# Top-32 attention and an expert layer: row scores as float32 products of two row halves, candidates in blocks, a new list

## The chip, the cores and the metric

The kernel runs on one core of a Trainium2 chip. The metric is the device time of one execution in microseconds, the median of several. TensorE (PE in the profile) multiplies, VectorE (DVE) finds the top 32, ScalarE (ACT) copies out of PSUM and computes exponentials, GpSimd (POOL) does the small and slow elementwise work, SyncE (SP) issues the transfers.

## What is computed

Two stages. The first is attention for 8 batches of 8 heads, 576 rows of 64 elements, in which each row keeps only its 32 largest scores; the second is a layer of four attention experts over the result, of which each row takes two.

```
scores = q @ k.T / 8;  kth = 32nd largest of each row
scores = where(scores >= kth, scores, -1e9);  x = softmax(scores) @ v      # per batch and head
logits = x @ w_gate;  sel = the two largest of 4;  w = softmax(sel)
out += [e in sel] * w * (causal_softmax(x wq_e (x wk_e).T / 8) (x wv_e)) wo_e   # per expert e
```

Which 32 scores a row keeps depends on their order, so the row scores are computed to nearly float32 precision.

## The kernel before

Two heads make a pair, and 32 pairs are worked off, four to a batch. The two heads of a pair have x = 0 and 1. Their 1152 rows are nine tiles of 128: tiles 0 to 3 are rows of head 0, 5 to 8 of head 1, and tile 4 holds the last 64 rows of head 0 and the first 64 of head 1.

**Preparation** (`prep`, from L684). One transfer brings q (partitions 0 to 63) and k (64 to 127) of both heads into `raw`. Each half is rounded to float32r (`cast`, ScalarE), the remainder is formed in place (`sub`, GpSimd), and copies on SP's queue (`dup1`, `dup2`, `again`) lay three operands of 128 partitions: q1 = [q low; q high], k1 = [k high; k low], q2 = [q high; q low], and k2 with k high again. In the first pair head 0 is loaded once more with q and k exchanged (`load_swap`), and ScalarE and VectorE make the operands. 16 products of zeros come first on TensorE (`warm`).

**Row scores** (`scores`, L805). For a tile q1' k1 + q2' k1, each in two PSUM banks: four float32r products of 128 partitions, 576 columns twice over; tile 4 needs eight, as gaps of zeros keep the heads apart. ScalarE copies the tile out (`copy`, L809).

**Top 32** (`topk`, L790). For three tiles at once VectorE takes the maximum and minimum of the two halves of a row (`f1`, `f3`), folds the maxima twice more (`f2`, `f4`), and so makes candidates: 72 maxima, 72 minima, and three times the eight largest of what else is left (`f5`, `f6`), 168 in all. Four rounds take the eight largest (`win`) and strike them out (`rep`), two over the 72, two over the 168. GpSimd computes the smaller ones of one fold (`lesser`, L839 and L840), copies the eighth of each of the three eights to a place behind (`tails`, L852), and prepares a test whether the candidates sufficed (`compare`, L898). ScalarE makes a mask from the 32nd value (L917).

**Statistics and tail** (`stats`, `tail`). Row maximum and logarithm of the sum are split in two, transposed (`s8`, L998), and sent by SP as two more rows into q2 (`s10`, L1003). Then the scores are computed again, transposed and masked (`st`), ScalarE's exponential follows (L1105), and `av` multiplies with V in plain float32, two column halves of 64 side by side. float32 products show as two records each in the trace, the other types as one.

**Expert layer** (`moe`, L1135), once for each batch. Its stages are spread among the pairs that follow; in the score stage (`s_stage`) the two experts of a group lie in partitions 0 to 63 and 64 to 127, and their products of 64 partitions are issued in turn.

**Order.** `add` (L138) enters each step with its engine, its guessed duration in ns, what it waits for and the buffers it takes. For the main part the steps are issued in the order of `ORDER` (L287), a list of step numbers written out; so each engine works in a fixed order, and what is not ready holds up all behind it on its engine. `TURNS` (L106) is the planner's table of what it costs TensorE, in ns, to go from one shape of product to another: L is 128 by 128, C two column halves, R two partition halves, M the masks, T transpositions, F and X other cases. Buffers are rings of fixed size (`Ring`): `raw` 1, operands 3 and 2, PSUM slots 3.

## Time and profile before

| what | value |
|---|---|
| median of 3 runs | 1146.33 us (1146.16 to 1147.42) |
| the profiled execution | 1148.72 us |
| its span in the profile | 1146.9 us |
| mean granted TensorE clock | 0.976 of full speed |
| DMA | 103.49 MB, of it 35.89 MB read from HBM |

The profile comes from one execution. Its span runs from the first instruction to the last; a little lies around it. Busy times of an engine are shares of that span; a busy TensorE is not TensorE at its peak, because products are pipelined and their ends are modelled. Starts are measured, so the distance from one start to the next says what a group of products takes. A product's own duration is longer than that distance.

### The profile page before, as it was taken

To read this page: it belongs to the slowest core of one execution; us is meant where nothing else is said; L and a number is where in the kernel's file an instruction comes from. 1 tells how busy PE (TensorE), PEld (TensorE's weight loads), DVE (VectorE), ACT (ScalarE), POOL (GpSimd) and SP (SyncE) were. 2 spreads that over 40 slices of the span, in tenths; PEclk is the share of its full clock that TensorE was granted. 3 is DMA by queue.
4 is the path that set the end of the run, shared out by engine and by line. 5 is a ranking of instruction groups with operands and counts; after the bars stand their busy time and mean duration, and the time that the engine had idled before them with its cause. 6 is when DMAs were issued, how large, how long until landed. Compare 5 with 4: busy or idle time off the path is not lost.

```text
span 1146.9 us, 27854 instructions
## 1 busy us (share of the span) xinstructions
PE 1063.6 (93%) x9046; PEld 904.6 (79%) x9046; DVE 1031.7 (90%) x4518; ACT 928.5 (81%) x1900; POOL 584.1 (51%) x967
## 2 busy tenths in 40 slices
PE   4488889998999999999999999999999989999997
PEld 3366678877889788887888878897888878887885
DVE  6999999998999999999999999999999999998022
ACT  4788868897888988889789888889888888888554
POOL 3765564544655556445554555554554545653211
PEclk7698999999999999999999999999999999999999
DMA  4334333334343334333433233333532433321101
GB/s 132 105 101 109 85 84 86 79 83 104 97 115 85 84 106 114 79 101 99 106 85 103 65 106 113 97 86 93 134 90 61 111 96 98 103 68 29 37 33 46
DMA packets 57654, 103.49 MB, mean 90 GB/s; under 512 B 11870, under 2 KB 19676, under 8 KB 57500
## 3 DMA queue, kind: packets, MB, share of 16 engines
q1 hardware_dynamic: 57340, 101.32, 33.7%
q8 instruction: 74, 1.21, 0.4%
q14 instruction: 80, 0.66, 0.2%
q10 hardware_dynamic: 160, 0.30, 0.1%
HBM read 35.89 MB, written 9.50 MB: 40 GB/s over the span
## 4 chain that ended last, share of the span: by engine, by line
PE 42%; DVE 33%; ACT 10%; DMA 6%; issue 4%; POOL 2%; SPq 2%; DVEq 0%; ACTq 0%; POOLq 0%
PE slot L531 33%; PE acc L531 7%; DVE top L857 7%; DVE cand L862 7%; DVE fa L822 4%; DVE cand L844 3%; DVE fb L825 2%; DVE fc L828 2%; ACT s L809 2%; ACT mask L917 2%; DVE cand L848 1%; PE slot L1378 1%; DVE cand L849 1%; DMA raw<-in_qk_dram 1%; DVE sm L1358 1%
## 5 line engine op out<-in xcount | busy, mean ns | idle before, releaser
L839 POOL TENSOR_TENSOR fc<-fa,fc 128x432 int32<-128x432 int32 x96 | 115.6, 1204 | 307.7 <-DVE cand L834 298.5
L857 DVE MAX8 top<-cand 128x8 f32<-128x72 f32 (+1 forms) x1152 | 247.0, 270 | 0.0
L917 ACT ACTIVATE mask<-s,top 128x576 bf16<-128x576 f32 x288 | 213.2, 769 | 31.5 <-DVE top L857 31.4
L531 PE MATMUL slot<-opa,opa 128*128 128x256 f32 (+3 forms) x984 | 198.4, 322 | 26.9 <-DMA opa<-raw 12.9
L862 DVE MATCH_REPLACE8 cand<-top,cand 128x72 f32<-128x72 f32 (+1 forms) x864 | 208.5, 251 | 0.0
L809 ACT ACTIVATE s<-slot 128x576 f32<-128x576 f32 x288 | 178.6, 649 | 32.0 <-PE slot L531 31.0
L1105 ACT ACTIVATE pt<-slot 128x576 f32<-128x576 f32 x288 | 183.4, 649 | 24.7 <-PE slot L531 18.9
L531 PE MATMUL slot<-opb,opb 128*128 128x320 f32 (+1 forms) x960 | 188.1, 312 | 6.7 <-ACT pt L1105 2.2
L531 PEld LDWEIGHTS slot<-opa,opa 128*128 128x128 f32 (+1 forms) x984 | 148.1, 196 | 44.1 <-issue 21.6
L531 PE MATMUL acc<-pt,vt 128*64 128x256 f32 (+3 forms) x1152 | 177.7, 413 | 5.3 <-DMA vt<-in_vL_dram 2.8
L531 PEld LDWEIGHTS slot<-opb,opb 128*128 128x128 f32 x960 | 143.8, 193 | 20.6 <-ACT pt L1105 5.0
L531 PEld LDWEIGHTS acc<-pt,vt 128*64 128x64 f32 (+1 forms) x1152 | 104.2, 143 | 44.1 <-issue 6.7
L531 PE MATMUL slot<-negi,mask 128*128 128x128 bf16 (+3 forms) x1632 | 119.5, 216 | 1.6 <-ACT pt L1105 0.8
L840 POOL TENSOR_TENSOR fa<-fa,fc 128x432 int32<-128x432 int32 x96 | 110.1, 1147 | 7.5
L822 DVE TENSOR_TENSOR fa<-s 128x864 f32<-128x864 f32 x95 | 105.1, 1106 | 9.4 <-ACT s L809 9.2
L844 DVE MAX8 cand<-fb 128x8 f32<-128x288 f32 x288 | 112.1, 445 | 0.4
L898 POOL TENSOR_TENSOR ind<-cand,top 128x513 bf16<-128x513 f32 x96 | 101.4, 1056 | 12.9 <-ACT ind L904 10.2
L825 DVE TENSOR_TENSOR fb<-s 128x864 f32<-128x864 f32 x95 | 106.4, 1120 | 0.5 <-ACT s L809 0.5
L531 PEld LDWEIGHTS <-mask 128*128 128x128 bf16 (+1 forms) x1632 | 80.3, 101 | 28.1 <-issue 14.1
L531 PE MATMUL slot<-opa,k2a 128*128 128x256 f32 (+1 forms) x320 | 69.7, 299 | 2.9 <-DMA opa<-stat 1.9
L862 DVE MATCH_VALUE_LOAD cand<-top,cand 128x8 f32 x864 | 67.6, 78 | 4.0 <-POOL cand L852 4.0
L531 PE MATMUL slot<-opb,k2b 128*128 128x320 f32 x320 | 68.8, 296 | 1.8 <-DMA opb<-stat 1.8
(189 smaller groups left out, 2132.0 us busy)
## 6 DMA issues: line engine op xcount, KB each, us to landing
raw<-in_qk_dram SPq DMA_DIRECT2D x31, 576.0 KB
opb<-raw SPq DMA_DIRECT2D x96, 144.0 KB
opa<-raw SPq DMA_DIRECT2D x93, 144.0 KB
vt<-in_vL_dram SPq DMA_DIRECT2D x32, 320.0 KB
opb<-opb SPq DMA_DIRECT2D x64, 144.0 KB
opa<-opa SPq DMA_DIRECT2D x62, 144.0 KB
k2a<-opa SPq DMA_DIRECT2D x32, 144.0 KB
k2b<-opb SPq DMA_DIRECT2D x32, 144.0 KB
```

Source lines behind the costliest of these rows:

```text
L531: nc.tensor.matmul(o, l, r, start=start, stop=stop, skip_group_check=True)
L809: nc.scalar.activation(s3.t[:, n], sl.t[:, o0:o0 + S], AF.Copy)
L822: v.tensor_tensor(out=fa.t, in0=s3.t[:, :, 0:288], in1=s3.t[:, :, 288:576], op=OP.max)
L825: v.tensor_tensor(out=fb.t, in0=s3.t[:, :, 0:288], in1=s3.t[:, :, 288:576], op=OP.min)
L839: nc.gpsimd.tensor_tensor(out=m, in0=r, in1=m, op=OP.subtract)
L840: nc.gpsimd.tensor_tensor(out=l, in0=l, in1=m, op=OP.add)
L844: v.max(out=c.t[:, n, 160:168], in_=fb.t[:, n])
L857: v.max(out=w.top.t[0][:, j, 8 * r:8 * r + 8], in_=c.t[:, n, 0:72 if r < 2 else 168])
L862: v.match_replace(out=src, in_values=src, imm_value=LOW, in_to_replace=w.top.t[0][:, j, 8 * r:8 * r + 8])
L898: nc.gpsimd.tensor_tensor(out=ind.t[:, 513 * g:513 * g + 513].rearrange("p (a n) -> p a n", a=3), in0=c.t, in1=m32[:, js[0]:js[0] + 3, 31: ...
L917: nc.scalar.activation(w.mask[j].t, s3.t[:, n], AF.Relu, bias=w.top.t[0][:, j, 31:32], scale=-1.0)
L1105: es[j] = add("ACT", act(S), lambda sl=sl, pt=pt, o0=o0: nc.scalar.activation(pt.t, sl.t[:, o0:o0 + S], AF.Exp, scale=0.125), [a], bufs=[s ...
```

## The change

The row scores no longer use the float32r operands. q and k are loaded twice: `raw`, now one buffer for each half and three of them, holds [q; k] and, by two more transfers, [k; q]. A tile's scores are two float32 products of 64 partitions: columns 0 to 287 in partitions 0 to 63 and columns 288 to 575 in partitions 64 to 127, each into a bank of its own; tile 4 has four, for two output halves as well. They wait for the loads alone. Casts, remainders and copies are still made, for `st` alone, with fewer copies, and the two other operands lose their gaps. The first pair goes the same way as the others, with 8 products of zeros in place of 16; the load of its head 1 and of the value weights wait for steps of the first head.

The candidates lie in three blocks of 56: 24 maxima, 24 minima, an eight. The last two rounds read 55 of each block, so the eighths stay where they are, and `tails` goes. `f4` and `lesser` become two steps each, and the small GpSimd steps of the statistics (`s7`) and of the expert layer (`g7`, `diag`, `c6`) two to four, with dependences of their own; their instructions stay. `TURNS` gets a shape Z for the new products, and `ORDER` is another list. The parts of the diff that count here:

```diff
@@ -103 +103 @@ TURNS, in ns, gets these entries
+ "LZ": 92.0, "MZ": 60.0, "CZ": 60.0, "TZ": 40.0, "FZ": 90.0, "RZ": 0.0, "ZL": 42.0,
+         "ZC": 49.0, "ZT": 48.0, "ZM": 20.0, "ZR": -50.0, "ZX": 42.0, "ZF": 40.0}
@@ -285,227 +286,244 @@ ORDER: 5308 numbers become 5710, all in a new order
...
-    RAW = ring("raw", [P, 2, S], FT, int(1))
-    OPS = [sets("opa", int(3), *[([P, 640], FR)] * 3),
-           sets("opb", int(2), *[([P, 640], FR)] * 3)]
+    RAW = ring("raw", [P, 2, S], FT, 3)
+    OPS = [sets(f"op{n}", 2, ([P, S], FR), ([P, 640], FR), ([P, S], FR)) for n in "ab"]
...
-    CAND = ring("cand", [P, 3, 171], FT, 2)
-    IND = ring("ind", [P, 1548], BF, 1)
+    CAND = ring("cand", [P, 3, 3, 56], FT, 2)
+    IND = ring("ind", [P, 1521], BF, 1)
@@ -687,82 +703,66 @@
         pl.due = p - D_PREP
         w.ops, w.k2 = [Buf(r) for r in OPS], [Buf(r) for r in K2]
         w.vt = Buf(VT)
-        raw = Buf(RAW)
+        w.raw = [Buf(RAW) for _ in range(2)]
         src = qk[b, i]
-        w.scores, w.k2d = {}, []
-        load = None
+        w.loads, w.k2d = [], []
+        a = None
         for x in range(2):
-            ops, k2 = w.ops[x], w.k2[x]
+            ops, k2, raw = w.ops[x], w.k2[x], w.raw[x]
             c = slice(OFF[x], OFF[x] + S)
-            first = start and x == 0
-            if load is None or start:
-                ls = slice(x, x + 1) if start else slice(0, 2)
-                def load_(ls=ls):
-                    nc.sync.dma_start(raw.t[:, ls], src[:, ls])
-                load = add("SP", 820 if start else 1640, load_, bufs=[raw], lat=500 if start else 0, prio=1)
-            def cast(x=x, c=c):
-                nc.scalar.activation(w.ops[x].t[2][:, c], raw.t[:, x], AF.Copy)
-            def sub(x=x, c=c, first=first):
+            def load_(x=x, raw=raw):
+                nc.sync.dma_start(raw.t[:, 0], src[:, x])
+            def swap_(x=x, raw=raw):
+                eng = nc.scalar if start and x == 0 else nc.sync
+                for r, z in ((hi, lo), (lo, hi)):
+                    eng.dma_start(raw.t[r, 1], src[z, x])
+            def cast(x=x, raw=raw):
+                nc.scalar.activation(w.ops[x].t[2], raw.t[:, 0], AF.Copy)
+            def sub(x=x, raw=raw):
                 q1, k1, q2 = w.ops[x].t
-                if first:
-                    for t, r in ((q1, lo), (k1, hi)):
-                        nc.vector.tensor_tensor(out=t[r, c], in0=raw.t[r, x], in1=ft(q2[r, c]), op=OP.subtract)
-                else:
-                    nc.gpsimd.tensor_tensor(out=raw.t[:, x], in0=raw.t[:, x], in1=ft(q2[:, c]), op=OP.subtract)
+                nc.gpsimd.tensor_tensor(out=q1, in0=raw.t[:, 0], in1=ft(q2), op=OP.subtract)
             def dup1(x=x, c=c):
                 q1, k1, q2 = w.ops[x].t
-                for t, d, r in ((q1, hi, lo), (k1, lo, hi)):
-                    nc.sync.dma_start(ft(t[d, c]), ft(q2[r, c]))
+                for t in (k1, w.k2[x].t):
+                    nc.sync.dma_start(ft(t[lo, c]), ft(q2[hi]))
             def dup2(x=x, c=c):
                 q1, k1, q2 = w.ops[x].t
-                for t, d, r in ((q1, lo, lo), (k1, hi, hi), (q2, hi, lo)):
-                    nc.sync.dma_start(ft(t[d, c]), raw.t[r, x])
-            def again(x=x, c=c):
-                nc.sync.dma_start(ft(w.k2[x].t[lo, c]), ft(w.ops[x].t[1][lo, c]))
-            a = add("ACT", act(S, False), cast, [load], bufs=[ops, raw], prio=2)
-            if first:
-                swap = Buf(PR[0])
-                def load_swap(x=x, swap=swap):
-                    for r, z in ((hi, lo), (lo, hi)):
-                        nc.scalar.dma_start(swap.t[r, 0:S], src[z, x])
-                def cast_swap(x=x, c=c, swap=swap):
-                    for t, r in ((0, hi), (1, lo)):
-                        nc.scalar.activation(w.ops[x].t[t][r, c], swap.t[r, 0:S], AF.Copy)
-                def low_again(x=x, c=c, swap=swap):
-                    q1, k1, q2 = w.ops[x].t
-                    nc.vector.tensor_tensor(out=q2[hi, c], in0=swap.t[hi, 0:S], in1=ft(q1[hi, c]), op=OP.subtract)
-                ls = add("ACT", 200, load_swap, bufs=[swap], lat=3000, prio=-5000)
-                add("ACT", 1300, table, prio=-4000)
+                nc.sync.dma_start(ft(k1[hi, c]), ft(q1[hi]))
+            def again(x=x):
+                q1, k1, q2 = w.ops[x].t
+                nc.sync.dma_start(ft(q1[hi]), ft(q2[lo]))
+            first = [a] if start and x else []
+            l1 = add("SP", 820, load_, first, bufs=[raw], prio=1, tag="load_first" if start and x == 0 else "load_")
+            if start and x == 0:
+                tb = add("ACT", 1300, table, prio=-6000)
+                l2 = add("ACT", 200, swap_, bufs=[raw], lat=3000, prio=-7000, tag="load_swap")
                 dummy = Buf(SLOT)
                 def warm():
-                    for _ in range(16):
+                    for _ in range(8):
                         mm(dummy.t[:, 0:512], zero[:, 0:128], zero[:, 0:512], start=True, stop=True)
                 add("PE", 3000, warm, bufs=[dummy], prio=-5000)
-                u = add("DVE", 2 * dve(S), sub, [a], bufs=[ops, raw], prio=2)
-                e = add("ACT", 2 * act(S, False), cast_swap, [ls], bufs=[ops, swap], prio=2)
-                z = add("DVE", dve(S), low_again, [u, e], bufs=[ops, swap], prio=2)
-                w.scores[x] = [u, e, z]
             else:
-                u = add("POOL", pool(S), sub, [a] + marks[max(3 * p - 5 + x, 0):][:1], bufs=[ops, raw], prio=2)
-                e = add("SP", 1300, dup1, [a], bufs=[ops], prio=1)
-                g = add("SP", 1950, dup2, [u, e], bufs=[ops, raw], prio=1)
-                w.scores[x] = [e, g]
+                l2 = add("SP", 820, swap_, first, bufs=[raw], prio=1)
+            w.loads.append([l1, l2])
+            a = add("ACT", act(S, False), cast, [l1] + ([tb] if start and x == 0 else []), bufs=[ops, raw], prio=2)
+            u = add("POOL", pool(S), sub, [a], bufs=[ops, raw], prio=2)
             pl.due += D_K2
-            w.k2d.append(add("SP", 650, again, w.scores[x], bufs=[ops, k2], prio=2))
+            e = add("SP", 1300, dup1, [a], bufs=[ops, k2], prio=1)
+            g = add("SP", 650, dup2, [u], bufs=[ops], prio=1)
+            h = add("SP", 650, again, [g], bufs=[ops], prio=2)
+            w.k2d.append([e, h])
             pl.due -= D_K2
-        w.v = add("SP", 910, lambda: nc.sync.dma_start(w.vt.t, vL[b, i]), bufs=[w.vt], lat=400, prio=3, tag="loadv")
+        w.v = add("SP", 910, lambda: nc.sync.dma_start(w.vt.t, vL[b, i]), [a] if start else [],
+                  bufs=[w.vt], lat=400, prio=3, tag="loadv")
         return w
-                o0 = 512 - split_of(j)
-                def scores(j=j, sl=sl, o0=o0):
-                    product(sl.t, o0, split_of(j), parts(w, j), (0, 2), (1, 1), True)
-                def copy(n=n, sl=sl, o0=o0, s3=s3):
-                    nc.scalar.activation(s3.t[:, n], sl.t[:, o0:o0 + S], AF.Copy)
-                need = w.scores[0] + w.scores[1] if j == 4 else w.scores[0 if j < 4 else 1]
-                a = add("PE", 560 if j != 4 else 1185, scores, need, bufs=[sl, s3] + used(w, j), prio=0)
+                def scores(j=j, sl=sl):
+                    for k, (c0, c1) in enumerate(halves(288)):
+                        r = slice(64 * k, 64 * k + 64)
+                        for x in ((0, 1) if j == 4 else (j // 5,)):
+                            raw = w.raw[x].t
+                            o = slice(64 * x, 64 * x + 64) if j == 4 else al
+                            z = slice(512, 576) if j == 4 and x == 0 else slice(0, 64) if j == 4 else \
+                                slice(j * P, j * P + P) if x == 0 else slice(64 + (j - 5) * P, 64 + (j - 4) * P)
+                            mm(sl.t[o, 224 + c0:224 + c1], raw[r, k, z], raw[r, 1 - k, c0:c1], start=True, stop=True)
+                def copy(n=n, sl=sl, s3=s3):
+                    nc.scalar.activation(s3.t[:, n], sl.t[:, 224:224 + S], AF.Copy)
+                xs = (0, 1) if j == 4 else (j // 5,)
+                need = [t for x in xs for t in w.loads[x]]
+                a = add("PE", 520 if j != 4 else 600, scores, need, bufs=[sl, s3] + [w.raw[x] for x in xs], prio=0,
+                        kind="ZZ")
                 cps.append(add("ACT", act(S), copy, [a], bufs=[sl, s3], prio=0))
...
             def f4(fc=fc, c=c):
-                l, r = fc.t[:, :, 0:72], fc.t[:, :, 72:144]
-                v.tensor_tensor(out=c.t[:, :, 0:72], in0=l, in1=r, op=OP.max)
-                v.tensor_tensor(out=c.t[:, :, 72:144], in0=l, in1=r, op=OP.min)
-            def lesser(fa=fa, fc=fc):
+                l, r = [fc.t[:, :, o:o + 72].rearrange("p n (k a) -> p n k a", k=3) for o in (0, 72)]
+                v.tensor_tensor(out=c.t[:, :, :, 0:24], in0=l, in1=r, op=OP.max)
+            def f7(fc=fc, c=c):
+                l, r = [fc.t[:, :, o:o + 72].rearrange("p n (k a) -> p n k a", k=3) for o in (0, 72)]
+                v.tensor_tensor(out=c.t[:, :, :, 24:48], in0=l, in1=r, op=OP.min)
+            def lesser(n, fa=fa, fc=fc):
...
-                    v.max(out=c.t[:, n, 144:152], in_=fa.t[:, n, 0:72])
-                    v.max(out=c.t[:, n, 152:160], in_=fa.t[:, n, 72:144])
-            def tails(c=c):
-                nc.gpsimd.tensor_copy(c.t[:, :, 168:171], c.t[:, :, 151:168:8])
+                    v.max(out=c.t[:, n, 0, 48:56], in_=fa.t[:, n, 0:72])
+                    v.max(out=c.t[:, n, 1, 48:56], in_=fa.t[:, n, 72:144])
             def win(r, c=c, js=js):
                 for n, j in enumerate(js):
-                    v.max(out=w.top.t[0][:, j, 8 * r:8 * r + 8], in_=c.t[:, n, 0:72 if r < 2 else 168])
+                    v.max(out=w.top.t[0][:, j, 8 * r:8 * r + 8], in_=c.t[:, n, :, 0:24 if r < 2 else 55])
...
-                    src = c.t[:, n, 0:72 if r < 2 else 168]
+                    src = c.t[:, n, :, 0:24 if r < 2 else 55]
...
-        return add("SP", 2200 if x == 0 else 600, s10, [t9], bufs=[st] + (w.ops if x == 0 else w.ops[1:]), prio=0)
+        return add("SP", 2200 if x == 0 else 600, s10, [t9] + [w.k2d[h][0] for h in range(x, 2)], bufs=[st] + (w.ops if x == 0 else w.ops[1:]), prio=0)
```

## Rows read from the trace of the kernel before

**Rows 1.** The page's busy times: us, share of the span, instructions.
```profile
PE 1063.6 (93%) x9046; PEld 904.6 (79%) x9046; DVE 1031.7 (90%) x4518; ACT 928.5 (81%) x1900; POOL 584.1 (51%) x967
```

**Rows 2.** Stretches: us, then PE, PEld, DVE, ACT, POOL busy, PEclk, DMA share, GB/s.
```profile
15.05:100.00 84.95, 52.01 (x353) 41.77 (x353) 83.66 (x383) 63.02 (x139) 53.80 (x66) 0.80 0.39 105
100.00:1000.00 900.00, 866.97 (x7456) 743.61 (x7456) 868.55 (x3846) 764.50 (x1545) 483.81 (x794) 0.99 0.37 96
...
1059.10:1146.90 87.80, 78.59 (x697) 67.00 (x697) 19.02 (x31) 45.66 (x105) 14.41 (x39) 0.97 0.12 38
15.05:1059.10 1044.05, 976.78 (x8327) 833.52 (x8327) 1006.10 (x4462) 877.00 (x1789) 564.39 (x907) 0.98 0.36 94
```

**Rows 3.** The page's chain that ended last, by engine.
```profile
PE 42%; DVE 33%; ACT 10%; DMA 6%; issue 4%; POOL 2%; SPq 2%; DVEq 0%; ACTq 0%; POOLq 0%
```

**Rows 4.** Timeline of the start: start, us, engine, line, what [idle before <-releaser].
```profile
7.17 0.68 ACT L739 ACTIVATE opa<-prs 64x576 fp32r<-64x576 f32 x1 [1.47 <-DMA prs<-in_qk_dram]
...
12.72 4.03 PE L531 MATMUL slot<-opa,opa 128*128 128x256 f32 x16 [5.61 <-DVE opa L713]
...
14.37 0.65 ACT L809 ACTIVATE s<-slot 128x576 f32<-128x576 f32 x1 [3.95 <-PE slot L531]
15.05 0.46 DVE L869 TENSOR_TENSOR fa<-s 128x288 f32<-128x288 f32 x1 [1.69 <-ACT s L809]
```

**Rows 5.** Timeline of PE, row scores and a stage of the expert layer.
```profile
333.45 0.70 PE L531 MATMUL slot<-opa,opa 128*128 128x256 f32 x4
333.98 0.70 PE L531 MATMUL slot<-opb,opb 128*128 128x256 f32 x4
334.51 0.69 PE L531 MATMUL slot<-opa,opa 128*128 128x256 f32 x4
335.14 0.55 PE L531 MATMUL slot<-qk,qk 64*128 64x128 f32 x6
```

**Rows 6.** Timeline of PE, a tile of row scores behind a mask.
```profile
353.50 0.78 PE L531 MATMUL slot<-opa,opa 128*128 128x256 f32 x4
354.11 0.96 PE L531 MATMUL slot<-qk,bd 128*128 128x288 f32 x6
```

**Rows 7.** Timeline of PE, the product with V of two tiles.
```profile
341.30 2.16 PE L531 MATMUL acc<-pt,vt 128*64 128x256 f32 x16
343.39 0.66 PE L1378 MATMUL slot<-identr,prs 128*128 128x128 f32 x4
```

**Rows 8.** Timeline of PE, a 64-partition stage of the expert layer.
```profile
384.23 0.97 PE L531 MATMUL slot<-qk,qk 64*128 64x512 f32 x6
385.13 0.28 PE L531 MATMUL slot<-tri,negi 128*128 128x128 bf16 x2
```

**Rows 9.** Waits: who <- whom: us in total, times, longest us.
```profile
PE slot L531 <- DMA opa<-raw: 12.9, 1, 12.9
...
DVE cand L862 <- POOL cand L852: 4.0, 4, 1.6
```

**Rows 10.** Groups of DVE by form: busy us, mean ns | idle before.
```profile
L857 DVE MAX8 top<-cand 128x8 f32<-128x168 f32 x576 | 152.1, 320 | 0.0
...
L857 DVE MAX8 top<-cand 128x8 f32<-128x72 f32 x576 | 95.2, 220 | 0.0
...
L828 DVE TENSOR_TENSOR fc<-fa 128x432 f32<-128x432 f32 x96 | 58.2, 606 | 2.4
L834 DVE TENSOR_TENSOR cand<-fc 128x216 f32<-128x216 f32 x96 | 36.3, 378 | 0.0
```

**Rows 11.** Timeline of PE behind VectorE's last work.
```profile
1069.81 3.08 PE L531 MATMUL slot<-ptm,v 128*64 128x128 f32 x60
...
1080.42 3.05 PE L531 MATMUL slot<-wo,qk 128*128 128x512 f32 x12
```

More of the change, by code (lines that the diff above doesn't have):

```diff
@@ L584, in blank @@
     def blank(eng, x, u):
-        for t in OPS[x].tiles[u]:
-            eng.memset(ft(t[:, gap(x)]), 0.0)
+        eng.memset(ft(OPS[x].tiles[u][1][:, gap(x)]), 0.0)
     def blank2(eng, x):
@@ L943, in softsum @@
         t = add("DVE", 250 if n == 5 else 350, s1, top + ([] if w.general else made), bufs=b1, prio=0)
-        t2 = add("POOL", 240, s2, [t], bufs=b1, prio=0)
+        t2 = add("POOL", 240, s2, top + ([] if w.general else made), bufs=b1, prio=0)
         t = add("ACT", act(32 * n, False), s3, [t], bufs=[st], prio=0)
@@ L1537, in moe @@
             add("SP", 730, store, [a], bufs=[o], lat=1100, prio=3)
-    counts, made, marks, pending, first_copies = [], [], [], [], []
+    counts, made, pending, first_copies = [], [], [], []
     def compare_last():
@@ L1590 @@
         blank_later()
-        marks.clear()
         with tc.For_i(0, B) as b:
```

109 lines of the change are left out of this document (61 added, 48 removed), and 459 rows, old and new, of the table ORDER.

## The prediction

> **What bounds the kernel now.** I read the busy times first. TensorE shows 93% and VectorE 90% of the span, GpSimd 51% [rows 1]: two engines are near full, and a share of the whole can't say which of them ends a stage last. The table of stretches can. From 15.05 us, VectorE's first maximum, to 1059.1 us, its last work on the top 32, VectorE is busy 1006.1 of 1044.05 us, so it idles 38 us. From 100 to 1000 us the two are alike: TensorE 867.0 and VectorE 868.6 of 900 us. In the last 87.8 us TensorE is busy 78.6 and VectorE 19.0: that is the last batch's expert layer and what is left over of the batch before [rows 2]. The chain of waits agrees: 42% of it is on TensorE, 33% on VectorE [rows 3]. So the time is three pieces: 15.05 us until VectorE can begin, 1044 us in which VectorE and TensorE set the pace together, 87.8 us of TensorE. Each part of the change is costed in the piece where it lies. Of what TensorE alone gains or loses in the middle I take half, since the idle there is shared about evenly (33.0 and 31.5 of those 900 us); what VectorE gains I take whole, as its idle is what the other engine leaves it.
>
> **The start.** The first row scores now wait for a load and a swapped load, casts on ScalarE, subtractions on VectorE, and start on TensorE at 12.72; the first copy is at 14.37 and the first maximum at 15.05. ScalarE had waited for the swapped load's second piece until 7.17 [rows 4]. Afterwards the products read the loads themselves, so 7.2 is when they can start. The 2.33 us from TensorE's start to the maximum stay: four float32r products of 288 columns on average become two side by side of 288 columns with four passes, the same 1152 column times at whatever clock is granted there. First maximum at 9.5: **-5.5 us**, whole, for VectorE has nothing else to wait for. Bounds: 0 (the second half's load, which now waits for the first cast, comes late for the next groups) and -7 (the load lands sooner with less beside it).
>
> **Row scores on TensorE.** Now four float32r products take 0.53 us (333.98 to 334.51); tile 4, which has eight, takes 333.45 to 334.51, 1.07 us [rows 5]. For 32 pairs of heads that is 256 x 0.53 + 32 x 1.07 = 170 us. Of the 288 tiles 120 stand in the list behind a mask, a transposition or a product in another tiling and take 0.08 us more or a little over (353.50 to 354.11 is 0.61 [rows 6]), which makes some 183 us. Afterwards a tile is two float32 products of 64 partitions and 288 columns. Float32 in four passes is seen in the product with V: its sixteen records carry 2304 columns, half of them for each column half of the array, and take 2.09 us; 2304 x 4 / 2.4 GHz / 2 is 1.92 [rows 7]. One tile so streams 288 x 4 / 2.4 GHz = 0.48 us if its halves run together. That 64-partition halves do, the expert layer shows: six records of 64x512 take 0.90 us, one after the other they would need 1.28 [rows 8]. But the same rows have the price of going to 64 partitions and back: 0.90 is 0.26 above the 0.64 of three pairs, and the four products ahead of such a stage take 0.63 (334.51 to 335.14) where 0.53 is usual [rows 5]: **0.36 us a visit**. In the new list the 288 tiles stand in 165 groups, 11 of them behind the expert layer's own 64-partition products. So 288 x 0.48 + (165 - 11) x 0.36 = 138 + 55 = 193 us against 183: **+10 us** of TensorE, half of it in the time, **+5**. The low bound are the planner's own figures in the diff, 0.52 a tile and 0.60 for tile 4 (152 us), and with its table of turns 15 us more over the new list than over the old: 167 us against its 181, -14. The high bound is 0.24 more a visit (rival two). I take the price from the 64-partition rows, the nearest there are. The Trainium skill speaks against the change here: "TensorEngine Tiling (Array Packing)", section Tiling Modes, has it that a change of tiling mode, unlike one of tile, drains the engine. The 0.36 us of this trace agree; by that rule every group pays on the way in and out, which is the sum below, while without it, by the diff's figures, the time would be rival one's.
>
> **Casts, subtractions and copies off the way of the scores.** In the middle: 0. This work is due eight pairs early (D_PREP), and the one long wait of a product for it is 12.9 us [rows 9], in the first 100 us, where VectorE is busy 83.66 of 84.95 us [rows 2] and covers it; without that cover it would cost its 12.9. Queues: SP issues 1 load and 12 copies a pair now, 2 loads, 4 swapped loads and 8 copies then, one more; the bytes stay (six pieces of 144 KB a half either way). New waits: a load waits for one of three raw buffers, and the statistics' rows (s10) for the copies dup1; behind either, later loads stand in SP's queue, and the scores wait for those. They are ahead by a pair or more, so 0; bound +5, as pair 1's swapped load of head 0 stands sixteenth in the queue.
>
> **Candidates.** Three blocks whose eighths are skipped: reads of 165 in place of 168. The step is (320 - 220) / 96 = 1.04 ns an element [rows 10]; 864 such instructions x 3 x 1.04 = **-2.7 us** on VectorE. The copy of eighths leaves GpSimd, and with it VectorE's waits for it: **-4.0 us** [rows 9]; GpSimd's own time was free. Runs of 24 in place of 72 I take as free: 216 elements in runs of 72 take 378 ns, 432 in runs of 144 take 606 [rows 10], 1.06 ns an element with no price of a run to be seen; up to 5 ns for each of some 2,200 instructions, +11 us, stay in the range.
>
> **Split GpSimd steps.** The same instructions with finer dependences: 0. GpSimd's idle half hides them; without it the statistics' transposition would be late, and all of TensorE's queue behind it.
>
> **The end.** Behind VectorE's last work TensorE still does some 12.6 us of batch 6: stages of its attention, products with V (3.0 us) and five outputs of about 1.4 us [rows 11]. In the new list two of the outputs (2.8 us) are left there: up to -10 us, if TensorE has room before. I take half: **-5**.
>
> **The sum.** -5.5 + 5 - 2.7 - 4.0 - 5 = -12.2 us against the profiled execution's own 1148.72 (its span 1146.9 and 1.8 around it): 1136.5. That execution stood 2.4 us above the median of 1146.33, so **1134**. A measurement of this kernel tells 0.2% (2.3 us) from no change.
>
> **Rivals.** One, *visits are cheap*: a turn costs what the diff's table says, TensorE gains 14 us, half of it counts, and all that is left over moves ahead: -5.5 - 7 - 2.7 - 4 - 10 = -29, 1117. For it, the list was made with these figures; against it, the 0.26 us inside [rows 8], of which the tile's 0.52 holds 0.04. 15%.
> Two, *slower*: a float32 product is two records, and if the second half of a tile starts only beside the first half's second record, every group streams 0.24 us longer: 165 x 0.24 = 40 us of TensorE, more than the 33 us it idles from 100 to 1000; all but half of that idle comes through: +23, 1157. It decides from 12.2 / 165 = 0.07 us a visit, if all of that comes through. For it: the code issues half by half. Against it: the product with V has the same order by columns and took 2.09 us [rows 7]; in strict order it would be 2.9. The Trainium skill, "TensorE: Matmul & The Clock Gate", Part 3, states that products start strictly in program order, by which this rival would hold; the 2.09 us disagree. 18%.
> Three, *hidden*: late loads, or VectorE's waits for TensorE, take back what the start and the end give; what stays is the candidates' 2.7 or nothing, 1142 to 1147. 15%.
> The forecast has 52%.
>
> **How the numbers follow.** The forecast and rival one are faster; of the third's 15, I put 7 to faster, 6 to within 0.2%, 2 to slower: faster 0.74, same 0.06, slower 0.20. The forecast's own range is 1124 (TensorE's 10 hidden, the end whole) to 1143 (nothing at the end, TensorE's 10 whole). For 8 in 10 it reaches just past rival one and short of rival two: 1115 to 1151.
>
> **What would show it.** Right: first maximum near 9.5 us; tiles 0.48 us apart within a group and about 0.85 alone; no copy of nine elements on GpSimd; maxima of 165 at 317 ns; batch 6 all but done when VectorE ends, near 1050 us. Wrong: halves that start more than a few ns apart, an idle of VectorE over 50 us in the middle, or visits without the 0.36.

## The result and the profile after

The changed kernel takes 1158.99 us (median of 4 runs, 1157.97 to 1161.16) where the one before, on the same chip, takes 1146.88 (1146.16 to 1148.07): ratio 1.0107, 95% interval 1.0089 to 1.0125, some 12 us slower. The forecast was 1134, its range 1115 to 1151: wrong, on the other side. The profiled execution took 1161.16 us with a span of 1159.4, where before it was 1148.72 with 1146.9.

The page's busy times, and the stretches as in [rows 1, 2]; the last starts at the first maximum and ends with the last sum over the top 32:

```profile
PE 1074.9 (93%) x9038; PEld 820.5 (71%) x9038; DVE 1032.1 (89%) x4511; ACT 929.9 (80%) x1897; POOL 586.3 (51%) x865
...
9.35:100.00 90.65, 57.61 (x398) 37.10 (x394) 87.52 (x402) 66.63 (x146) 56.19 (x66) 0.78 0.40 106
100.00:1000.00 900.00, 866.30 (x7353) 664.03 (x7353) 850.94 (x3740) 752.98 (x1518) 476.93 (x693) 0.99 0.34 93
1078.71:1159.39 80.68, 68.31 (x593) 57.68 (x592) 15.89 (x27) 39.61 (x90) 9.23 (x29) 0.96 0.09 29
9.35:1078.71 1069.36, 1000.00 (x8428) 759.41 (x8424) 1013.67 (x4466) 887.04 (x1804) 572.32 (x822) 0.97 0.35 93
```

In the kernel before the last sum over the top 32 ends at 1057.9 (the 1059.1 of [rows 2] is a maximum of the expert layer behind it), so by this mark its pieces are 15.05, 1042.85 and 89.0 us. The pieces at both ends got shorter, the start by 5.7 us and the tail by 8.3. The piece between them grew by 26.5, from 1042.85 to 1069.36. Some of that is the work that left the tail; but VectorE's idle in it grew from 36.8 (1042.85 - 1006.10) to 55.7 us (1069.36 - 1013.67), and that is where the loss is seen. An idle of over 50 us in the middle is one of the signs that the prediction named for being wrong.

The start, as in [rows 4]; the timelines of PE and of DVE:

```profile
6.34 6.30 PE L549 MATMUL slot<-raw 64*128 64x288 f32 x28 [1.53 <-DMA raw<-in_qk_dram]
...
30.94 3.25 PE L549 MATMUL slot<-raw 64*128 64x288 f32 x12 [16.65 <-DMA raw<-in_qk_dram]
```
```profile
9.35 1.42 DVE L877 TENSOR_TENSOR fa<-s 128x288 f32<-128x288 f32 x3 [5.81 <-ACT s L815]
```

The first maximum stands at 9.35, as forecast. The next pair's first product stands at 30.94: TensorE waits 16.65 us for its load. In the kernel before it stood at 33.30, after the 12.87 us that are [rows 9]'s wait. So 2.4 of the 5.7 us are left by then.

Score tiles in the middle, timeline of PE (as [rows 5, 6]):

```profile
399.56 0.76 PE L549 MATMUL slot<-raw 64*128 64x288 f32 x4
400.24 1.66 PE L549 MATMUL slot<-wo,qk 128*128 128x512 f32 x6
401.83 0.76 PE L549 MATMUL slot<-raw 64*128 64x288 f32 x4
402.52 1.67 PE L549 MATMUL slot<-wo,qk 128*128 128x512 f32 x6
404.12 0.72 PE L549 MATMUL slot<-raw 64*64 64x288 f32 x8
404.76 0.53 PE L549 MATMUL acc<-x,negr 128*128 128x256 f32 x2
```

A tile by itself takes 0.68 to 0.69 us from its start to the next one's (399.56 to 400.24), and the products beside it keep the engine some 0.1 us longer on either side (the six records with wo take 1.59 to 1.60 us between two tiles, 1.50 behind a tile alone, and as little as 1.40 with none beside them). Within a group tiles follow at 0.48. The two halves of a tile start 7 ns apart (401.834 and 401.841).

VectorE's waits, who <- whom: us in total, times, longest us; first before, then after:

```profile
DVE fa L822 <- ACT s L809: 9.2, 13, 1.2
DVE cand L862 <- POOL cand L852: 4.0, 4, 1.6
...
DVE stat L975 <- ACT stat L971: 3.8, 3, 2.2
```
```profile
DVE fa L830 <- ACT s L815: 18.9, 17, 6.5
DVE stat L985 <- ACT stat L981: 9.9, 13, 3.1
...
DVE fb L833 <- ACT s L815: 4.7, 8, 1.8
DVE cand L860 <- POOL fa L852: 3.9, 10, 0.9
```

The wait for GpSimd's copy is gone, but VectorE waits longer for the copies of the scores (18.9 + 4.7 where 9.2 and 0.5 for fb) and for the softmax sums' exponentials (9.9 where 3.8). These two together, called **the copies and sums** from here on, grew from 13.5 to 33.5 us.

**TensorE's work and waits.** All starts of matmul records were put to their tasks. What a task takes up to the next task's start is its work, as far as it is usual (the lowest fifth) for that kind of task between those neighbours; the rest is waiting. It is an estimate, and where the usual is drawn moves it by some us. By it TensorE has 1011.6 us of work and 126.4 of waits before, 1020.9 and 126.7 after. Without the warming products at the start (11.5 and 5.1) the work grew by **15.7 us**: the tiles fell from 183.4 to 171.0, and their neighbours rose by 28 (the products with V of [rows 7] by 7.0, the statistics' transposes by 5.9, the attention stages by 4.7). The waits did not shrink.

**TensorE's waits for copies of q and k.** The row scores no longer need these copies, but the second computation of the scores (`st`) does. From 100 us on, timeline of PE, and VectorE's next maximum behind the second of these waits:

```profile
102.16 0.82 PE L549 MATMUL slot<-opa,opa 128*128 128x256 f32 x2 [4.87 <-DMA opa<-opa]
...
716.24 0.82 PE L549 MATMUL slot<-opb,opb 128*128 128x320 f32 x2 [3.45 <-issue]
```
```profile
728.06 1.06 DVE L830 TENSOR_TENSOR fa<-s 128x864 f32<-128x864 f32 x1 [6.53 <-ACT s L815]
```

Both times TensorE starts some 0.1 us after the landing of the last copy of a half (`again`): issued at 99.69 and landed at 102.02; issued at 710.16, behind a load of V, an output and the next load, and landed at 716.15. The profile's line names nobody for the second wait; the landing is in the trace's record of the copy's semaphore. Together that is 8.3 us, where in the kernel before TensorE's waits for such copies sum to 2.1 us from 100 us on (1.1 and 1.0, the longest 1.1). Behind the second wait the granted clock is 0.62 in the next 8.2 us, in which VectorE's longest wait of the piece begins:

```profile
716.20:724.40 8.20, 8.16 (x44) 7.33 (x44) 5.34 (x38) 2.51 (x3) 2.47 (x2) 0.62 0.31 83
```

### The profile page after: what moved, and what is told of

Read it like the earlier page. It is cut to its first block, busy times and chain, and to the rows that moved or that the text cites. A ratio compares the mean times of both kernels' runs of the same rounds, so it can differ in the third digit from the quotient of the medians.

```text
span 1159.4 us, 27659 instructions
## 1 busy us (share of the span) xinstructions
PE 1074.9 (93%) x9038; PEld 820.5 (71%) x9038; DVE 1032.1 (89%) x4511; ACT 929.9 (80%) x1897; POOL 586.3 (51%) x865
## 5 line engine op out<-in xcount | busy, mean ns | idle before, releaser
L865 DVE MAX8 top<-cand 128x8 f32<-128x165 f32 (+1 forms) x1152 | 245.4, 269 | 0.6
L850 POOL TENSOR_TENSOR fc<-fa,fc 128x432 int32<-128x432 int32 x96 | 110.8, 1154 | 238.7 <-DVE cand L844 164.8
L549 PE MATMUL slot<-raw 64*128 64x288 f32 (+1 forms) x1280 | 199.5, 453 | 29.8 <-DMA raw<-in_qk_dram 18.2
L549 PEld LDWEIGHTS slot<-raw 64*128 64x128 f32 (+1 forms) x1280 | 95.4, 182 | 93.5 <-issue 38.4
L549 PEld LDWEIGHTS acc<-pt,vt 128*64 128x64 f32 (+1 forms) x1152 | 99.9, 142 | 54.4 <-issue 19.6
L907 POOL TENSOR_TENSOR ind<-cand,top 128x504 bf16<-128x504 f32 x96 | 111.6, 1163 | 47.0 <-DVE top L865 24.7
L830 DVE TENSOR_TENSOR fa<-s 128x864 f32<-128x864 f32 x95 | 104.9, 1104 | 19.2 <-ACT s L815 18.9
L549 PE MATMUL slot<-opa,opa 128*128 128x256 f32 (+5 forms) x344 | 81.3, 329 | 5.7 <-DMA opa<-opa 5.2
L549 PE MATMUL slot<-opb,opb 128*128 128x320 f32 x320 | 75.6, 318 | 3.8 <-issue 3.5
L1001 POOL TENSOR_TENSOR stat<-stat 128x5 f32<-128x5 f32 x64 | 17.8, 279 | 100.3 <-ACT stat L995 96.0
```

Source lines behind the costliest of these rows:

```text
L549: nc.tensor.matmul(o, l, r, start=start, stop=stop, skip_group_check=True)
L830: v.tensor_tensor(out=fa.t, in0=s3.t[:, :, 0:288], in1=s3.t[:, :, 288:576], op=OP.max)
L850: nc.gpsimd.tensor_tensor(out=m, in0=r, in1=m, op=OP.subtract)
L865: v.max(out=w.top.t[0][:, j, 8 * r:8 * r + 8], in_=c.t[:, n, :, 0:24 if r < 2 else 55])
L907: nc.gpsimd.tensor_tensor(out=ind.t[:, 504 * g:504 * g + 504].rearrange("p (a n) -> p a n", a=3), in0=c.t.rearrange("p a k n -> p a (k n)" ...
```

## Experiments

Theory A at first: TensorE sets the pace from about 100 us on, so its 15.7 us come through whole and VectorE's savings don't count. The rivals were B (VectorE sets the pace), C (each counts half) and D (the new list itself is slow).

**Blocks alone, in the kernel before.**

```diff
-                v.tensor_tensor(out=c.t[:, :, 0:72], in0=l, in1=r, op=OP.max)
+                v.tensor_tensor(out=c.t[:, :, :, 0:24], in0=l, in1=r, op=OP.max)
...
-                nc.gpsimd.tensor_copy(c.t[:, :, 168:171], c.t[:, :, 151:168:8])
+                pass
```

> The kernel before, its own list and its own score products, with the candidates in three blocks: maxima and replacements of 165 elements where they were of 168 and 171, nothing copied by GpSimd in front of the third round. Worth 2.7 us of instructions and up to 4.0 us of waits on VectorE. Theory A (TensorE sets the pace from about 100 us on, so what VectorE saves does not come through): 1145 to 1148 us, no difference. Theory B (VectorE sets the pace, its savings come through whole, as the prediction counted them): 1140 us. Theory C (each engine counts half): 1143.5 us.

1136.72 us against 1145.41: ratio 0.9919 (0.9902 to 0.9935), 9.3 us faster by the ratio (8.7 by the medians), more than any theory gave, and faster than both kernels. A falls in its plain form. Then the copy's absence alone:

> The kernel before with the candidates side by side as they were, 168 to a row, and without GpSimd's copy of the three eighths' ends: the test for rows with too few candidates leaves these three values out. If the 8.7 us of the blocks alone are the waits around the copy: 1137 to 1139 us. If they are the shorter rows (2.7 us of instructions): 1144 to 1146 us.

1139.62 against 1146.57: 0.9942 (0.9923 to 0.9960), 6.6 us. Most of the gain is the copy. Waits for and of the copy in the kernel before, on GpSimd and in SP's queue:

```profile
POOL cand L852 <- DVE cand L862: 21.8, 11, 4.0
...
SPq L725 <- POOL cand L852: 34.1, 10, 11.7
```

GpSimd stood at the copy for 21.8 us until VectorE had its eighths, with the statistics and the subtractions behind it in its queue, and SP's queue stood 34.1 us behind that. What TensorE's weight load for the statistics' transposes waited for, before and with the blocks alone:

```profile
L998 PEld LDWEIGHTS slot<-identr,stat x64: 83/85/89, 44.7 to 1061.6; 128*10 128x10 f32 x32, 128*8 128x8 f32 x32
...
  POOL stat L992: 24.4, 15
```
```profile
L997 PEld LDWEIGHTS slot<-identr,stat x64: 82/85/89, 43.8 to 1050.3; 128*10 128x10 f32 x32, 128*8 128x8 f32 x32
...
  POOL stat L991: 16.7, 10
```

TensorE's work is the same 1011.7 with the blocks, its waits fell by 11.3 to 115.1. The shorter rows are there too: VectorE's busy total fell by 9.2 us, 2.0 of it on the maxima of 165 (152.1 to 150.1) and 4.1 on the 95 maxima of halves, whose mean fell from 1106 to 1063 ns without the copy on GpSimd beside them.

**Less work for VectorE**, in the changed kernel and in the one before:

```diff
-                    v.max(out=c.t[:, n, 2, 48:56], in_=fb.t[:, n])
+                    v.max(out=c.t[:, n, 2, 48:56], in_=fb.t[:, n, 0:144])
```

> The changed kernel, but the eight largest of the minima are looked for in the first 144 of each row's 288 minima only (the other half of the minima is left out): 288 maxima of about 0.295 us where they take 0.445 us, 43 us less work on VectorE. Theory A: VectorE only gets a wider margin, 1152 to 1160 us. Theory B: up to 43 us faster, 1116 to 1125 us. Theory C: about 1138 us.

> The kernel before, but the eight largest of the minima are looked for in the first 144 of a row's 288 minima only (half of the minima is left out): 43 us less work on VectorE, with the old list. Theory A (TensorE's own work and its waits add up to the time; VectorE counts only where TensorE waits for it): 1133 to 1141 us, since only some 10 of TensorE's waits can be VectorE's. Theory B (VectorE sets the pace in the old list): 1103 to 1115 us. If the old list is like the changed kernel's in this, 2 to 3 us.

1156.74 us, some 2 less than the changed kernel (0.2%, inside the intervals), and 1141.59 against 1146.57, 0.9954 (0.9935 to 0.9972), 5 us less. VectorE's busy total fell by 38 us in both (to 994.5 and 993.4). B falls with either list: what VectorE saves by itself turns into its idle.

**More work for TensorE**, in the kernel before:

```diff
+                    x, r, t = parts(w, j)[0]
+                    mm(sl.t[:, o0:o0 + 128], t[0][:, r], t[1][:, OFF[x]:OFF[x] + 128], start=True, stop=True)
```

> The kernel before with its own list, and one more float32r product of 128 partitions and 128 columns ahead of each of the 288 score tiles, whose result is overwritten: about 0.055 us each, 15 to 16 us more work on TensorE and nothing else. Theory A: 15 us slower, 1160 to 1164 us. Theory C: 1154 to 1155 us. Theory B: 1147 to 1149 us.

1160.52 against 1145.41: 1.0128 (1.0111 to 1.0145), 15 us. That looks like A, but the work added was not 15: by the starts TensorE's work is 1041.9, 30 us more (0.105 us a product), and its waits fell by 20. So half of it came through: C, and the prediction's half.

**Without 64-partition products, in the new list.** A first try with float32r products that waited for their casts took 1227.76 us (TensorE waited for casts, ScalarE 80.5 us for tiles) and answers nothing:

> The changed kernel with its own list, loads and blocks, but a score tile is four float32r products of 128 partitions and 288 columns, as many columns as before the change, so no product of 64 partitions is left among the scores. They read the rounded q and k twice, so the scores are other numbers than the reference's, the branch for rows with too few candidates is never taken, and a tile waits for its cast too (24 tiles stand a little later in the list for that). Theory A (the switches to 64 partitions cost about 61 us where the shorter streaming saves 45, and all of it comes through): 16 us less than the changed kernel, 1142 to 1147 us. Rival D (the new list or the loads are what is slow, whatever the products): within 3 us of the changed kernel's 1159. Theory C: 1151 us.

Then float32 products of 128 partitions straight from the loads:

```diff
-                            mm(sl.t[o, 224 + c0:224 + c1], raw[r, k, z], raw[r, 1 - k, c0:c1], start=True, stop=True)
+                        for k, n in ((0, 288), (1, 48)):
+                            mm(sl.t[o, 224:224 + n], raw[:, k, z], raw[:, 1 - k, 0:n], start=k == 0, stop=k == 1)
```

> The changed kernel with its own list, loads, waits and buffers, but a score tile is two float32 products of 128 partitions, 288 and 48 columns (four passes a column, so 0.56 us, what a tile took before the change), and the copy reads the 288 columns twice: no product of 64 partitions is left among the scores. The scores are other numbers, half of the columns are left out, and the branch for rows with too few candidates is never taken. Theory A (what the changed products add to TensorE's own work, 15.7 us by the two traces, comes through whole): 1142 to 1146 us. Rival D (the products cost nothing in the end, the new list or the loads are slow): 1156 to 1160 us.

> The changed kernel with its own list, loads and waits, but a score tile is one float32 product of 128 partitions and 288 columns, which the copy reads twice (other numbers, half of the columns left out, and the branch for rows with too few candidates is never taken). By the run with 336 columns (0.68 us a tile, 21 us more work on TensorE than the changed kernel) a tile is now 0.54 us and TensorE has 21 us less work than the changed kernel's, 5 less than the kernel before. Theory F (with the new list TensorE's work comes through whole): 1137 to 1141 us. Theory C (half, as in the kernel before with the extra product): 1148 to 1150 us. Rival D (the new list's own waits take its place): 1155 to 1160 us.

> The changed kernel with its list and loads, but a score tile is one float32 product of 128 partitions and 335 columns (the copy reads 288 of them twice: other numbers, columns left out, the branch for rows with too few candidates never taken): by the runs with 288 and with 288 and 48 columns TensorE's work is then 1005 us, the changed kernel's less the 15.7 us that the 64-partition products add. Theory F (that work comes through whole): 1143 us. Theory C (half): 1151 us. Rival D: 1156 us or more.

| run | TensorE's work, waits | time | copies and sums |
|---|---|---|---|
| 288 and 48 columns | 1041.7, 124.3 | 1179.83 | 40.4 |
| changed kernel | 1020.9, 126.7 | 1158.99 | 33.5 |
| 335 columns | 999.8, 139.8 | 1154.23 | 27.5 |
| 288 columns | 980.3, 145.4 | 1138.12 | 20.3 |

Within a group the tile of 288 and 48 columns took 0.71 us, not 0.56, so the first of these is a run with more work; the others remove 21.1 and 40.6. More work comes through whole; of the first 21 us taken away 4.8 come back by the medians (3.4 by the ratios, 8.7 by the spans of the profiled executions), of 40.6 some 21. VectorE's waits in the run with 335 columns, to be held against those of after:

```profile
DVE fa L829 <- ACT s L813: 15.1, 14, 3.7
DVE stat L984 <- ACT stat L980: 9.2, 12, 3.1
...
DVE fb L832 <- ACT s L813: 3.2, 7, 0.8
```

With 21.1 us less work, and no switch, the waits for the copies of the scores are 5.3 us shorter in sum (18.3 for 23.6). The ratios, 1.0077 and 1.0107, lie so close that their intervals touch; that the products alone cost time is shown by the next run. But with less work on TensorE than before (999.8 for 1011.6, of which 6.4 are warming products) this kernel still is 0.8% slower than before (1.0054 to 1.0100): D, or the staging, holds too.

The same run tells what the price of a visit hangs on. Timeline of PE, the same stretch of the list as in the rows from 399.56 on above:

```profile
398.16 1.81 PE L549 MATMUL slot<-wo,qk 128*128 128x512 f32 x6
399.80 0.72 PE L549 MATMUL slot<-raw 128*128 128x335 f32 x2
400.11 1.82 PE L549 MATMUL slot<-wo,qk 128*128 128x512 f32 x6
```

From one group with wo to the next it is 1.95 us here, 1.40 for wo and 0.55 for the tile, which is what 335 columns in four passes stream (335 x 4 / 2.4 GHz = 0.56). In the changed kernel it is 2.28 (400.24 to 402.52): 1.40, 0.48 and 0.40. So a float32 tile of 128 partitions pays nothing for standing alone, and the 0.40 belong to the 64 partitions, not to the type.

**The products alone, in the old list.**

```diff
-                    product(sl.t, o0, split_of(j), parts(w, j), (0, 2), (1, 1), True)
+                            l, rr, h = ((t[2], t[1], lo), (t[0], t[1], hi))[k]
+                            mm(sl.t[o, 224 + c0:224 + c1], ft(l[h, z]), ft(rr[h, OFF[x] + c0:OFF[x] + c1]), start=True, stop=True)
```

A first form, with other operands in half of the columns, took the branch for rows with too few candidates and did the work again (4184.06 us), so only its first pass can be read: its last maximum of the top 32 ends at 1071.3 us, where before it ended at 1055.2, some 16 us later. The expectation that follows for the next form was worked out from 1059.7, where the last but one of the groups of three tiles ends.

> The kernel before with its own list, casts, copies and candidates, but every score tile is made as in the change, two float32 products of 64 partitions over 288 columns each at once, from the rounded q and k that lie in both halves (the low parts of q and k are left out of the scores). The old list has 186 groups of score tiles where the new one has 165: by the new list's 15.7 us for 165 groups, 186 groups cost some 23 us more work on TensorE than the old products. If half of it comes through, as with the extra product (30 us of work, 14 us of time): 1157 to 1159 us. If all of it: 1168 to 1170 us. If the products cost nothing by themselves: 1146 to 1149 us.

The same with the branch never taken:

> The kernel before with its own list, casts, copies and candidates, but every score tile is made as in the change, two float32 products of 64 partitions over 288 columns each at once, from operands that lie in both halves (the rounded q and k, and for the second half of the columns the rounded q and k's low part: other numbers), and the branch for rows with too few candidates is never taken. If the first pass of the run before tells it: 4 to 6 us slower than before, 1150 to 1152 us, which with the 5 us in the new list says that the products cost some 5 us in either. If half of an estimated 23 us of work comes through: 1157 to 1159 us. If they cost nothing: 1144 to 1148 us.

1160.90 against 1146.78: 1.0119 (1.0100 to 1.0139), **13.6 us slower**, from the products alone. TensorE's work grew by 21.3 us for 186 groups, its waits fell by 8.3. The copies and sums grew from 13.5 to 26.5, by 13.0, near the time that was lost. The expectation read from the first pass was too low, since it took the wrong maximum for the last; the one from half the work was about right.

**The blocks undone in the changed kernel.**

```diff
             def win(r, c=c, js=js):
+                if r == 2:
+                    nc.gpsimd.tensor_copy(c.t[:, :, 168:171], c.t[:, :, 151:168:8])
```

(and the candidates side by side again).

> The changed kernel with the candidates side by side again, 168 and 171 to a row, and with GpSimd's copy of the three eighths' ends, issued just ahead of the third round; everything else stays. Theory F (with the new list VectorE and GpSimd have room, so the blocks are worth nothing there): 1158 to 1162 us. If the blocks are worth in the new list what they are in the old one: 1167 to 1169 us.

1166.69: 1.0179 (1.0157 to 1.0201) against 1.0107, some 8 us. The blocks are worth in the new list what they are in the old.

**The start**, taken out of the changed kernel, and added to the blocks in the kernel before:

```diff
-                    for _ in range(8):
+                    for _ in range(42):
```

> The changed kernel with 42 instead of 8 warming products, so that the first score tile starts some 6 us later, near 12.5 us, as in the kernel before. If the early start is worth what the first maximum shows: 1164 to 1165 us. If only what the second batch's first product shows (30.9 us in the changed kernel, 33.3 in the one before): 1161 to 1162 us. If nothing: 1158 to 1160 us.

1161.41 (1.0142, 1.0114 to 1.0170; first maximum at 14.33): 2.4 us by the medians, 4.0 by the ratios, 0.4 by the spans of the profiled executions. The second pair's first product moved too, from 30.94 to 35.95, so both marks went back by 5.0 us and the time by less than either. VectorE still is 2.7 us behind at 716 us; then it waits 3.84 us at the place where the changed kernel waits 6.53, and from there on the two profiled executions run level:

```profile
728.09 1.06 DVE L830 TENSOR_TENSOR fa<-s 128x864 f32<-128x864 f32 x1 [3.84 <-ACT s L815]
```

> The kernel before with its own list and products, with two parts of the change: the blocks without copies (1136.7 us by themselves), and the first three score tiles as float32 products of 64 partitions straight from the loaded q and k, with their copies and maxima moved ahead of the first casts in the list. First maximum near 9.5 us where it is 15.05. Theory A (the start comes through whole): 1130 to 1132 us. Rival E (the start is hidden, what stands behind waits for the casts anyway): 1135 to 1138 us.

> The kernel before with the blocks and with the first three score tiles from the loaded q and k, once more with more rounds. If the start adds its 3 us (first product of the second batch at 30.1 us where it was 33.3) to the blocks' 9: ratio 0.989 to 0.990, 1133 to 1135 us. If it adds nothing: ratio 0.992, 1137 us.

0.9924 (0.9896 to 0.9952) and 0.9911 (0.9891 to 0.9930) for this kernel, with the first maximum at 8.51 and the second pair's first product at 29.54; the blocks alone gave 0.9919. What the start adds, 0.6 us lost in one and 0.9 won in the other, is within the intervals. A third form, with the first pair's subtractions on GpSimd, made the second pair later (40.17 us) and took 1140.94:

> The kernel before with the blocks and the early first three tiles, and the first half's three subtractions on GpSimd instead of VectorE, the load of the second batch ahead of the repeated k in SP's queue. First maximum near 8.7 us, first product of the second batch near 27 us where it is 33.3 in the kernel before and 30.1 with the early tiles alone. If the start counts by the second batch's first product: 6 us less than the blocks alone, about 1131 us. If the start is hidden behind later waits: 1136 to 1138 us.

So in the old list a start is not worth the 6 us that the first maximum shows, and no run here separates its worth from the 2 to 4 us of the second pair's first product or from nothing.

**The changed code in the old order.**

```diff
-3 2 0 140 1 4 10 5 19 9 17 20 21 18 46
+2 1 3 0
```

(the whole list, each old task replaced by the one of its name).

> The changed kernel, all of its code, products, loads and blocks, but in the order of the old list: each old task's place is taken by the changed kernel's task or tasks of the same name (the copies of eighths drop out; 163 tasks, nearly all of them casts, subtractions and copies of q and k on SP, ScalarE and GpSimd, stand later than in the old list, where their buffers come free); TensorE's order is the old one without exception. Score tiles then stand alone 70 more times. Rival D (the new list by itself is slow): well under the changed kernel's 1159, 1140 to 1150 us. Theory F (the products are what is slow, whatever the list): 1156 us or more, since there are more switches.

1232.28 us (1.0765, 1.0726 to 1.0805). D as put, that the old order would be better, is wrong. SP's queue here and in the changed kernel, longest sums of waits (L723 and L732 are the first copies of k, dup1):

```profile
SPq L723 <- PE slot L540: 368.5, 36, 19.5
```
```profile
SPq L732 <- PE slot L549: 207.7, 30, 20.5
```

In the kernel before the longest such sum, of one line for one engine, is 82.3 us, at the second copy of k. dup1 now fills the second copy too, whose one buffer TensorE holds until the pair before is through, and what stands behind it in the queue waits. With two such buffers (and two of the loads instead of three):

> The changed kernel in the order of the old list, as in the run with 1232 us, but with two buffers for each half's second copy of k where there was one, and two for the loaded q and k where there were three. The copies of k then stand late in the list in 27 places where they did in 62. If it is the second copy of k, made together with the first one, that holds up SP's queue and with it the casts and the tail: 1160 to 1180 us. If it is the order itself or the operands' two buffers: 1215 us or more.

1220.63: these buffers are not it, or not alone; the queue then stands 321.1 us at the loads. Nor does the queue as a whole wait longer in the changed kernel: its waits sum to 734 us before, 723 in the changed kernel and 789 in the old order. dup1's own waits are 189 us before, for casts above all, and 209 in the changed kernel, for TensorE. Why the changed staging can't keep the old order, and how much of it is the two operand buffers of head 0 where there were three, stays open.

## Why the prediction was wrong

**The start** was right at the first maximum (9.35 for 9.5) and mis-sized as a term: -5.5 became some -2.4 by the medians (0.4 to 4.0 by other measures). The second pair's load makes TensorE wait 16.65 us, and a wait that both share later takes more of it. "VectorE has nothing else to wait for" held for one pair only.

**Row scores.** The price was right: 0.48 in a group, and alone 0.69, which with the 0.1 each of the task ahead and the task behind is near the forecast's 0.85; 0.37 to 0.40 us a visit for 0.36. The work grew by 15.7 for a forecast of 10. Half of it was to count; measured were 13.6 of 21.3 in the old list and 4.8 of 21.1 in the new one, so of 15.7 some 4 to 10 us for the forecast's 5. The term had the right sign and mechanism, and was about right or too small. In "Tiling Modes" the Trainium skill, "TensorEngine Tiling (Array Packing)", says that a change of mode drains the engine; the 0.40 us that a tile of 64 partitions pays, and one of 128 does not, agree.

**Candidates** gave -9.3 and some -8 for -6.7, but not by "what VectorE gains I take whole": 38 us off VectorE gave 5 and 2. Most of it (6.6 of the 9.3) came because GpSimd no longer stands at the copy with the statistics behind it. "GpSimd's own time was free" was right, its place in the queue was not.

**The end.** Tail work moved ahead as forecast, but the -5 never showed by itself; the work lies in a piece that grew by 26.5 us. The upper end of the forecast's own range, without this term and with TensorE's 10 whole, adds up to 1144, not to 1143.

**The step that failed** is the 0 for the casts, subtractions and copies, and with it a sum that prices parts and takes the new order as neutral. By the single runs the start is -2.4, the blocks some -8 and the products 4 to 10, together some -6 to 0 if they add up, and measured are +12. So 12 to 18 us came with the new staging and the new order, at a point where the forecast had put 0 and a bound of +5. The bound was worked out for the loads that the scores wait for. The trace shows what it left out: the second computation of the scores still needs the copies, and TensorE waits for the last of them 4.87 us at 102.16 and 3.45 us at 716.24, the second time with a granted clock of 0.62 behind it and VectorE's longest wait of the piece. These 8.3 us are a part of the 12 to 18. No run moves these copies alone, so their share of the time, and where the rest lies, in the list or in the buffers, stays open; the runs in the old order show only that the changed code needs another list.

**Rivals.** Rival two's time (1157) came near by luck, its mechanism is refuted: the halves start 7 ns apart. The Trainium skill's "TensorE: Matmul & The Clock Gate", Part 3, has products start in program order, and in the same part it has products of different row tiles overlap, with starts some 4 ns apart; the 7 ns agree with both, so the rival did not follow from that page as the prediction had it. Rival one, cheap visits, falls by the 15.7 us. Rival three saw half of it: late loads did take back most of the start.

## What to carry to other kernels

Price a switch of tiling mode on TensorE by its visits, not by the tile: by the prediction's sum the tiles' own time fell by 45 us (183 to 138), and 165 visits at 0.37 to 0.40 us took more than that back. Where two engines are near 90%, saving work on one of them is worth little; look for the short instruction on a third engine that waits in an in-order queue with the path's work behind it (9 elements a row were worth 7 us). When a consumer is freed of some copies, look for the other consumer that still needs them. And a hand-written order is a part of the change with a price of its own: change the code in the old order first, one part at a time. The blocks alone, 1136.72 us, beat both kernels.

## What was not expected of the hardware

A product costs far more than its columns when it is short: a float32r product of 128 columns took 0.105 us (tiles in a group follow at 0.637 us with it and at 0.53 without). In float32 tiles follow at 0.485 us with 288 columns, at 0.563 with 335 and at 0.708 with 288 and 48: 0.22 for 48 columns in a product of their own, and 0.08 for 47 more in the same product. The 48 are added to sums that the product just ahead wrote, and what part that has is not tested. The groups of the runs with 48 and with 335 columns:

```profile
L549 PE MATMUL slot<-raw 128*128 128x288 f32 x512 | 189.0, 454 | 26.6 <-DMA raw<-in_qk_dram 18.4 <-ACT pt L1120 3.6 <-ACT s L814 2.4
L549 PE MATMUL slot<-raw 128*128 128x48 f32 x512 | 83.7, 246 | 0.0
```
```profile
L549 PE MATMUL slot<-raw 128*128 128x335 f32 x512 | 187.4, 478 | 28.0 <-DMA raw<-in_qk_dram 18.7 <-ACT pt L1119 4.2 <-ACT s L813 3.1
```

And VectorE's maxima of halves got shorter, 1106 to 1063 ns, when GpSimd no longer had its small copy, with the same operands and shapes; the least of them take 1.03 us in either kernel. In the changed kernel, without the copy but with another list, they are back at 1104:

```profile
L822 DVE TENSOR_TENSOR fa<-s 128x864 f32<-128x864 f32 x95 | 101.0, 1063 | 10.9 <-ACT s L809 10.7
```
```profile
L830 DVE TENSOR_TENSOR fa<-s 128x864 f32<-128x864 f32 x95 | 104.9, 1104 | 19.2 <-ACT s L815 18.9
```

The first line is of the kernel with the blocks alone, the second of the changed kernel. What runs on GpSimd beside them is the list's choice. In the traces the maxima with no GpSimd instruction beside them average 1.05 us in all three kernels, and those over 1.2 us, 7 in the kernel before, 2 with the blocks alone and 11 in the changed kernel, all have one. By the Trainium skill, "SBUF — State Buffer", section SBUF: two separate sides, VectorE with two inputs and GpSimd, when it reads SBUF, take a shared pair of ports in turns, whole instructions at a time; these traces agree (1.48 us at 20.64 in the changed kernel, beside a subtraction on GpSimd from 19.80 on), though no run here sets out to test it.
